# Retention and a spatial-gating block on one core: steps of batches 0 to 2 in another order

## The chip, the core and the metric

The kernel runs on one core of one Trainium2 chip. The core has five engines with a queue of instructions each: TensorE (PE in the profile) for matrix products, VectorE (DVE), ScalarE (ACT), GpSimd (POOL), and SyncE (SP), which here only issues transfers. They wait for each other through semaphores. The metric is the time of one execution in microseconds; before the change its median over three runs is 555.22 us (555.17 to 558.64).

## The reference

Two blocks follow each other. `x` of the second is the output of the first.

```python
# first: q, k, v of (8 batches, 8 heads, 576, 64)
scores = scale * np.matmul(q, k.transpose(0, 1, 3, 2))
Dmat = np.where(rel >= 0, gamma[:, None, None] ** rel[None, :, :], 0.0)
out = np.matmul(scores * Dmat[None], v)                  # rel = i - j, gamma per head
# second: x of (8, 576, 512)
h = np.maximum(x @ w_in, 0.0)
u, v = (h[..., :512], h[..., 512:])
v_n = (v - mean(v)) / np.sqrt(var(v) + 1e-06)            # over the last axis
v_s = np.einsum('ts,bsd->btd', w_spatial, v_n) + b_spatial[None, :, None]
result = (u * v_s) @ w_out
```

## The kernel before, in words

The eight batches go through five stages. **Retention** (`retention(b)`) works a batch in four chunks of 128 positions and a tail of 64: `scores` forms a chunk's products of q and k on TensorE and multiplies them by the decay on VectorE (`at`); `burst` runs the state products, the next chunk's scores and the products with v on TensorE and updates the state `st`; `evac` splits the chunk into a high and a low half in `x`; `prep` scales the keys and queries of a chunk on GpSimd (`qkv`, `qsc`). **v** (`v_steps`) forms five row blocks of v (block 4 is the tail) and normalises each: Relu on ScalarE, statistics on VectorE, the standard deviation and the centring on ScalarE, its inverse on VectorE, the high half of vn on ScalarE, the low half on VectorE. **u** (`u_stage`) forms eight tiles of 128 x 288 with a Relu on ScalarE. **vs** (`vs_stage`) multiplies vn by w_spatial, eight tiles of 14 matmuls, and gates them with u on VectorE. **f** (`f_stage`) multiplies by w_out, eight tiles, which ScalarE copies to `o` and SyncE stores.

Every operand exists as a high and a low half, so each product is three matmuls (`mm3`). The weights come in 64-bit words and are converted while the first batches run: `front` (ScalarE's absolute value and GpSimd's max), `mid` (three operations on VectorE: a shift and two combines on the whole tile `f`), `back` (ScalarE's high half, GpSimd's low half). Kinds 0, 1 and 2 are the u half of w_in, its v half, and w_out, in four pieces each. w_spatial comes as fp32 and is split by `w_sp_steps`: four `wsp` pieces, a cast on ScalarE and a subtraction on GpSimd each, and a last step for the tail (`wtl`), two of each.

Results of TensorE go to PSUM. Two banks (`r`) serve the retention in turn. All other tiles share the pool `ps_m` with four buffers (line 41): a tile holds its buffer from its first matmul to the last operation that reads it, for a v block that is the low half of vn.

What sets the order is of two sorts. Up to `ordered[0] = False` (line 639) the order is written out by hand: generators for v blocks, mids and splits are advanced step by step with `go`, between calls of `scores`, `burst`, `evac`, `prep` and `load`. In this part lie retention of batches 0 and 1, v of batch 0, then for batch 0 vs ahead of u (tile vs (0,0) is gated with `pre`, the Relu of the two u tiles of block 0 that are formed first). Behind it a scheduler places the instructions of each engine by its own times; the program gives it v and u of batch 1, with one step of `wout_work` (front, mid or back of w_out's pieces 2 and 3) at each tile, then f of batch 0, then from `interleave` (line 461) the rest of batch 1 beside the retention of batch 2, and so on with each batch beside the next one's retention. Each engine then runs its queue in that order and waits at an instruction whose input is not ready.

Of the kernel before, what the change touches and what calls it, by code (L numbers as in the profile page):

```python
# [18 lines left out]
B, H, S, D = 8, 8, 576, 64  # L19
# [8 lines left out]
NMB = DM // P  # L28
# [5 lines left out]
def retention_gmlp(ctx, tc, qkv, q_x, qk_t, q_xt, v_t, w_in, w_sp, b_sp, w_out, amask, qscale, kdec, sdec, out):  # L34
# [20 lines left out]
    def slot(name):  # L55
        return cp.tile([P, 2, NCB, S], F32R, name=name, tag="slot", bufs=2)
# [44 lines left out]
    def pair():  # L101
        banks.reverse()
        return banks[0]
# [84 lines left out]
    def front(kind, i, clamp=po):  # L188
        words = staged[kind, i].rearrange("p (n two) -> p n two", two=2)
        hw, lw = words[:, :, 1], words[:, :, 0]  # L190
        f = early[:, i] if kind == 1 else sp.tile([P, 512], F32, name=f"f_{kind}{i}", tag="f", bufs=3)
        a = f if clamp is po else ps_m.tile([P, 512], F32, name=f"w_{kind}{i}", tag="m")
        ac.activation(out=a, in_=hw.bitcast(F32), func=AF.Abs)
        if clamp is po:
            po.tensor_scalar(out=a, in0=a, scalar1=2.0 ** -15, scalar2=None, op0=ALU.max)
        part[kind, i] = hw, lw, a, f
# [15 lines left out]
    def mid(kind, i):  # L212
        for _ in mid_steps(kind, i):
            pass

    def back(kind, i, eng=po):
        hi, lo = (w[:, i, DH:] if kind == 1 else w[:, :, i * P:(i + 1) * P] for w in (win if kind < 2 else wout))
        f, ps = (t if kind == 1 else t.rearrange("p (a n) -> p a n", a=NCB) for t in part[kind, i])
        ac.copy(out=hi, in_=ps)
        if eng is po and kind == 1:  # L220
            ac.copy(out=f, in_=ps)
        eng.tensor_tensor(out=lo, in0=f if eng is po else ps, in1=hi.bitcast(F32), op=ALU.subtract)
# [15 lines left out]
    xs = {}  # L238

    def mm(out, w, r, start, stop):  # L240
        tc.keep_in_program_order(pe.matmul(out, w, r, start=start, stop=stop))
# [4 lines left out]
    def rows(c):  # L246
        return C if c < NC else TL
# [4 lines left out]
    def side(p, i):  # L252
        return i ^ (p % 2)

    def scores(b, c):
        n = rows(c)
        q, k, _, _ = chunk[b, c]
        ps = pair().rearrange("p i (a n) -> p i a n", a=NP)
        for s in range(n // D):
            for p, i in heads:  # L260
                mm(ps[half[s ^ side(p, i)], i, p, s * D:n], k[half[i], p, half[s]], q[half[i], p, s * D:n], True, True)
        a = wk.tile([P, 2, NP, C], F32, name=f"at_{b}_{c}", tag="at")
        ve.tensor_tensor(out=a[:, :, :, :n], in0=ps[:, :, :, :n], in1=am[:, :, :, :n], op=ALU.mult)
        at[b, c] = a

    def prep(b, c):
        n = rows(c)
        if c < NC:
            kh = chunk[b, c][2].rearrange("p (h d) -> p h d", h=H)
            po.tensor_tensor(out=kh, in0=kh, in1=kd.broadcast_to([P, H, D]), op=ALU.mult)  # L270
        if c > 0:
            t = qsc[b, c][:, :, :n]
            po.tensor_tensor(out=t, in0=t, in1=qs[:, :, :n], op=ALU.mult)
# [40 lines left out]
    def evac(b, c):  # L314
        src = xo[b, c]
        t = slice(c * C, c * C + rows(c))
        hi, lo = ((xs[b][:, i, :, t] if c < NC else xt[:, :, i]).rearrange("p (a j) n -> p j a n", j=2) for i in range(2))
        ac.copy(out=hi, in_=src)
        ve.tensor_tensor(out=lo, in0=src, in1=hi.bitcast(F32), op=ALU.subtract)
        if c == NC:  # L320
            po.tensor_copy(out=xs[b][:, :, :, t], in_=xt.rearrange("p a i n -> p i a n"))

    def retention(b):
        if b not in xs:
            xs[b] = slot(f"x_{b}")
        nxt = [(b, c) for c in range(NC + 1)] + [(b + 1, c) for c in range(2)]
        if (b, 0) not in at:
            prep(b, 0)
            scores(b, 0)
        yield 0.95  # L330
        for c in range(NC + 1):
            nx = nxt[c + 1] if nxt[c + 1][0] < B and (b, c) != (1, NC) else None
            if nx:
                prep(*nx)
            burst(b, c, nx)
            evac(b, c)
            if nxt[c + 2:] and nxt[c + 2][0] < B and nxt[c + 2] not in chunk:
                load(*nxt[c + 2])
            yield 2.65

    def mm3(ps, w, r, start, stop):
        pe.matmul(ps, w[0], r[0], start=start, stop=False)
        pe.matmul(ps, w[0], r[1], start=False, stop=False)
        pe.matmul(ps, w[1], r[0], start=False, stop=stop)
# [52 lines left out]
    def u_mm(b, db, t, ps):  # L397
        x = xs[b]
        ts = slice(t * HALF, (t + 1) * HALF)
        for cb in range(NCB):  # L400
            mm3(ps, [win[i][:, cb, db * P:(db + 1) * P] for i in range(2)], [x[:, i, cb, ts] for i in range(2)], cb == 0, cb == NCB - 1)
# [4 lines left out]
    def u_tile(b, db, t):  # L406
        ps = ps_m.tile([P, 512], F32, name=f"u_{b}_{db}_{t}", tag="m")[:, :HALF]
        u_mm(b, db, t, ps)
        u_relu(b, db, t, ps)

    def u_stage(b):
        for db in range(NDB):
            for t in range(2):
                u_tile(b, db, t)
                yield 1.6

    def v_stage(b):
        for sb in range(NC + 1):
            v_block(b, sb)
            yield 2.75 if sb < NC else 1.9  # L420
# [20 lines left out]
    def f_stage(b, g):  # L441
        for t in range(2):
            ts = slice(t * HALF, (t + 1) * HALF)
            for mb in range(NMB):
                o = wk.tile([P, HALF], F32, name=f"o_{b}_{mb}_{t}", tag="o", bufs=4)
                ps = ps_m.tile([P, 512], F32, name=f"f_{b}_{mb}_{t}", tag="m")[:, :HALF]
                for db in range(NDB):
                    mm3(ps, [wout[i][:, db, mb * P:(mb + 1) * P] for i in range(2)], [g[:, i, db, ts] for i in range(2)], db == 0, db == NDB - 1)
                ac.copy(out=o, in_=ps)
                sy.dma_start(out=out[b, mb * P:(mb + 1) * P, ts], in_=o)  # L450
                yield 1.6

    def main(b):
        if b > 1:
            yield from v_stage(b)
            yield from u_stage(b)
        g = slot(f"g_{b}")
        yield from vs_stage(b, g)
        yield from f_stage(b, g)

    def interleave(a, r, ta, tr):
        da = dr = 0.0
        a, r = iter(a), iter(r)
        la = lr = True
        while la or lr:
            if lr and (not la or dr / tr <= da / ta):
                try:
                    dr += next(r)
                except StopIteration:
                    lr = False  # L470
            elif la:
                try:
                    da += next(a)
                except StopIteration:
                    la = False

    def go(gen, n=1):
        for _ in range(n):
            next(gen)
# [32 lines left out]
    v = [v_steps(0, sb) for sb in range(NC + 1)]  # L512
    m = [mid_steps(0, i) for i in range(NDB)]
    sps = w_sp_steps()
# [11 lines left out]
    burst(0, 3, None)  # L526
    go(m[0])
    evac(0, 3)
    go(v[1])
    scores(0, NC)  # L530
    go(v[1])
    go(sps, 2)
    go(v[2], 2)
    burst(0, NC, None)
    evac(0, NC)
    go(v[2])
    go(m[0])
    back(0, 0)
    load(1, 1)
    fetch(2, 0)  # L540
    prep(1, 0)
    go(sps)
    go(v[3])
    go(v[4])
    go(v[3])
    go(v[2], 2)
    go(v[4])
    go(v[3])
    go(sps)
    ret = retention(1)  # L550
    xs[1] = slot("x_1")
    scores(1, 0)
    go(v[4])
    go(v[3])
    go(sps)
    u = cp.tile([P, NDB, S], F32, name="u", tag="u")
    pre = cp.tile([P, NDB, DM], F32, name="pre", tag="wout1")
    for t in range(2):
        ps = ps_m.tile([P, 512], F32, name=f"u_0_0_{t}", tag="m")[:, :HALF]
        u_mm(0, 0, t, ps)  # L560
        ac.activation(out=pre[:, t, :HALF], in_=ps, func=AF.Relu)
        go(v[4 - t])
    go(v[4])
    go(v[3])
    go(ret)

    def vs_tile(t, db):
# [52 lines left out]
    gated_u(1, 1)  # L620
    gated_u(1, 2)
    go(ret)
    mid(2, 1)
    gated_u(1, 3)
    back(2, 1)
    split_g(1)

    def wout_work():
        for i in range(2, NMB):
            front(2, i)  # L630
            yield
            mid(2, i)
            yield
            back(2, i)
            yield

    work = wout_work()
    g0 = xs[0]
# [1 line left out]
    for eng in (pe, ve, ac, po):  # L640
        ctx.enter_context(tc.issue_after(eng.last))

    for stage in (v_stage(1), u_stage(1)):
        for _ in stage:
            next(work, None)
    for _ in f_stage(0, g0):
        pass
    for b in range(1, B):
        interleave(main(b), retention(b + 1) if b + 1 < B else [], 50.0 if b > 1 else 26.1, 12.5 if b > 1 else 13.25)


_OUT = (B, DM, S)
# [74 lines left out]
```

## Time and profile before

| | |
|---|---|
| median of 3 runs | 555.22 us |
| the profiled execution | 555.62 us |
| its span, first to last instruction | 553.70 us |
| TensorE, matmuls busy | 536.8 us (97%) |
| VectorE busy | 269.0 us (49%) |
| ScalarE busy | 207.4 us (37%) |
| GpSimd busy | 133.9 us (24%) |
| mean granted TensorE clock | 0.988 |

Nearly all instructions are issued through one helper, so the profile gives line 71 for them; they are told apart by the names of their tiles (`vs<-wsp,vn` is a matmul of the vs stage that reads wsp and vn). Times are in us from the start of the span. TensorE's clock is given as a share of its full speed. The rows below are of one execution, on its own clock.

### The profile page before, as it was taken

To read this page: it belongs to the slowest core of one execution; us is meant where nothing else is said; L and a number is where in the kernel's file an instruction comes from. 1 tells how busy PE (TensorE), PEld (TensorE's weight loads), DVE (VectorE), ACT (ScalarE), POOL (GpSimd) and SP (SyncE) were. 2 spreads that over 40 slices of the span, in tenths; PEclk is the share of its full clock that TensorE was granted. 3 is DMA by queue.
4 is the path that set the end of the run, shared out by engine and by line. 5 is a ranking of instruction groups with operands and counts; after the bars stand their busy time and mean duration, and the time that the engine had idled before them with its cause. 6 is when DMAs were issued, how large, how long until landed. Compare 5 with 4: busy or idle time off the path is not lost.

```text
span 553.7 us, 15312 instructions
## 1 busy us (share of the span) xinstructions
PE 536.8 (97%) x6735; PEld 498.0 (90%) x6735; DVE 269.0 (49%) x588; ACT 207.4 (37%) x447; POOL 133.9 (24%) x133
## 2 busy tenths in 40 slices
PE   6897999899999999999999999999999999999997
PEld 4676998799998899989999899988999899998997
DVE  7685566922643735247351654327353373506240
ACT  4356323742223632236222551226322362226422
POOL 4747557700212111202112120121201122000000
PEclk8898899999999999999999999999999999999999
DMA  8992465002464322533225222342225342020002
GB/s 318 381 310 80 162 193 191 0 22 76 164 180 146 105 80 67 201 118 102 50 96 182 78 96 50 128 150 89 88 55 180 114 149 49 2 76 11 2 1 86
DMA packets 37045, 64.08 MB, mean 116 GB/s; under 512 B 14833, under 2 KB 27249, under 8 KB 33010
## 3 DMA queue, kind: packets, MB, share of 16 engines
q1 hardware_dynamic: 36978, 63.10, 34.5%
q8 instruction: 53, 0.87, 0.7%
q14 instruction: 14, 0.11, 0.1%
HBM read 53.65 MB, written 9.44 MB: 114 GB/s over the span
## 4 chain that ended last, share of the span: by engine, by line
PE 85%; DMA 5%; DVE 5%; ACT 3%; issue 1%; POOL 1%; SPq 0%; ACTq 0%; DVEq 0%
PE vs L71 21%; PE f L71 19%; PE u L71 17%; PE v L71 14%; PE r L71 14%; DMA qkv<-in_qkv 5%; DVE f L71 2%; DVE s L71 1%; ACT x L71 1%; DVE sm L71 1%; ACT vn L71 0%; POOL qsc L71 0%; DVE vn L71 0%; DVE w L71 0%; POOL qkv L71 0%
## 5 line engine op out<-in xcount | busy, mean ns | idle before, releaser
L71 PE MATMUL vs<-wsp,vn 128*128 128x288 f32 x768 | 115.6, 299 | 3.0 <-ACT pre L71 2.4
L71 PEld LDWEIGHTS vs<-wsp,vn 128*128 128x128 f32 x768 | 105.9, 189 | 4.9 <-ACT pre L71 2.7
L71 PE MATMUL u<-x,win 128*128 128x288 f32 x768 | 105.6, 296 | 2.2 <-ACT u L71 2.2
L71 PEld LDWEIGHTS u<-x,win 128*128 128x128 f32 x768 | 103.0, 188 | 3.7 <-POOL f L71 2.5
L71 PE MATMUL v<-win,x 128*128 128x512 f32 x384 | 93.3, 398 | 0.0
L71 PE MATMUL f<-g,wout 128*128 128x288 f32 x672 | 92.3, 296 | 0.0
L71 PEld LDWEIGHTS f<-g,wout 128*128 128x128 f32 x672 | 89.8, 188 | 0.5
L71 DVE TENSOR_TENSOR at<-r,am 128x1024 f32<-128x1024 f32 (+1 forms) x40 | 44.5, 1113 | 94.0 <-PE r L71 94.0
L71 PEld LDWEIGHTS v<-win,x 128*128 128x128 f32 x384 | 71.0, 188 | 16.6
L71 POOL TENSOR_TENSOR qsc<-qsc,qs 128x512 f32<-128x512 f32 (+1 forms) x31 | 36.1, 1165 | 177.5 <-DMA qsc<-in_q_x 112.7
L71 PEld LDWEIGHTS r<-qkv 64*64 64x64 f32 x2176 | 47.3, 139 | 14.0 <-issue 6.6
L71 PE MATMUL r<-qkv 64*64 64x64 f32 (+1 forms) x2176 | 54.0, 240 | 4.6 <-POOL qkv L71 2.8
L71 DVE BATCH_NORM_STATS2 s<-v 128x6 f32<-128x512 f32 (+1 forms) x40 | 27.7, 693 | 60.3 <-ACT v L71 59.3
L71 ACT COPY o<-f 128x288 f32<-128x288 f32 x64 | 25.6, 400 | 72.0 <-PE f L71 71.9
L71 ACT CAST g<-vs 128x288 fp32r<-128x288 f32 x56 | 22.3, 399 | 75.8 <-DVE vs L71 75.8
L71 ACT CAST x<-r 128x512 fp32r<-128x512 f32 x32 | 18.8, 586 | 60.0 <-DVE st L71 60.0
L71 POOL TENSOR_TENSOR qkv<-qkv,kd 128x512 f32<-128x512 f32 x32 | 33.3, 1043 | 32.3 <-DMA qkv<-in_qkv 25.1
L71 DVE TENSOR_TENSOR g<-vs,g 128x288 fp32r<-128x288 f32 x56 | 25.6, 458 | 26.3 <-ACT g L71 26.3
L71 PE MATMUL r<-at,qkv 64*64 64x64 f32 (+1 forms) x1152 | 37.6, 228 | 0.4 <-DVE at L71 0.4
L71 POOL TENSOR_TENSOR st<-st,sd 128x256 f32<-128x256 f32 x24 | 14.9, 620 | 93.4 <-DVE st L71 93.4
L71 DVE TENSOR_TENSOR vs<-vs,u 128x288 f32<-128x288 f32 x56 | 26.0, 464 | 23.0 <-PE vs L71 23.0
L71 PEld LDWEIGHTS r<-at,qkv 64*64 64x64 f32 (+1 forms) x1152 | 32.1, 141 | 2.8 <-DVE at L71 0.6
(73 smaller groups left out, 509.6 us busy)
## 6 DMA issues: line engine op xcount, KB each, us to landing
qkv<-in_qkv SPq DMA_DIRECT2D x31, 1024.0 KB, 5.3
out<-o SPq DMA_DIRECT2D x64, 144.0 KB, 1.8
qsc<-in_q_x SPq DMA_DIRECT2D x24, 256.0 KB, 3.2
raw_v<-in_w_in SPq DMA_DIRECT2D x4, 512.0 KB, 6.5
qkv<-in_qk_t SPq DMA_DIRECT2D x8, 256.0 KB, 3.2
qkv<-in_v_t SPq DMA_DIRECT2D x16, 128.0 KB, 3.4
raw<-in_w_in SPq DMA_DIRECT2D x4, 512.0 KB, 8.4
raw<-in_w_out SPq DMA_DIRECT2D x4, 512.0 KB, 4.1
```

Source lines behind the costliest of these rows:

```text
L71: ins = op(*args, **kw)
```

## The change

Three things move; no instruction's work changes. First, in the part written by hand: the `wsp` splits and the `wtl` step of w_spatial are advanced earlier, the last steps of v blocks 2, 3 and 4 of batch 0 come in another order, the key scaling of chunk 0 of batch 1 (`prep(1, 0)`) comes later, and that chunk's `scores` move behind the two first u tiles. Second, mid and back of w_out's piece 1 leave the part written by hand, and pieces 1 to 3 now advance with the u tiles of batch 1 alone, no longer from the v blocks on. Third, `main(1)` begins with f of batch 0, so the retention of batch 2 is interleaved with f of batch 0, vs and f of batch 1, instead of the last two.

```diff
     def main(b):
-        if b > 1:
+        if b == 1:
+            yield from f_stage(0, g0)
+        else:
             yield from v_stage(b)
             yield from u_stage(b)
...
     evac(0, 3)
+    go(sps, 2)
     go(v[1])
     scores(0, NC)
     go(v[1])
-    go(sps, 2)
     go(v[2], 2)
     burst(0, NC, None)
     evac(0, NC)
     go(v[2])
+    go(sps)
     go(m[0])
     back(0, 0)
     load(1, 1)
     fetch(2, 0)
-    prep(1, 0)
-    go(sps)
     go(v[3])
     go(v[4])
     go(v[3])
-    go(v[2], 2)
+    go(v[2])
+    go(sps)
+    go(v[4])
+    go(v[2])
+    prep(1, 0)
+    go(v[3])
+    go(sps)
     go(v[4])
     go(v[3])
-    go(sps)
-    ret = retention(1)
-    xs[1] = slot("x_1")
-    scores(1, 0)
-    go(v[4])
-    go(v[3])
-    go(sps)
...
         u_mm(0, 0, t, ps)
+        if t:
+            go(v[4])
+            go(v[3])
         ac.activation(out=pre[:, t, :HALF], in_=ps, func=AF.Relu)
-        go(v[4 - t])
     go(v[4])
     go(v[3])
+    ret = retention(1)
+    xs[1] = slot("x_1")
+    scores(1, 0)
     go(ret)
...
     go(ret)
-    mid(2, 1)
     gated_u(1, 3)
-    back(2, 1)
     split_g(1)

     def wout_work():
-        for i in range(2, NMB):
-            front(2, i)
-            yield
+        for i in range(1, NMB):
+            if i > 1:
+                front(2, i)
+                yield
             mid(2, i)
             yield
             back(2, i)
...
-    for stage in (v_stage(1), u_stage(1)):
-        for _ in stage:
-            next(work, None)
-    for _ in f_stage(0, g0):
+    for _ in v_stage(1):
         pass
+    for _ in u_stage(1):
+        next(work, None)
     for b in range(1, B):
-        interleave(main(b), retention(b + 1) if b + 1 < B else [], 50.0 if b > 1 else 26.1, 12.5 if b > 1 else 13.25)
+        interleave(main(b), retention(b + 1) if b + 1 < B else [], 50.0 if b > 1 else 40.0, 12.5)
```

At two places the engines' order is shown as it stands in the built program. The first is ScalarE at the end of v of batch 0, just before vs tile (0,0). In the names, `v_3` and `v_4` are the v blocks in PSUM, `mv` and `sm` their statistics, `vt` the tail block of vn, `vn_343` the high half of vn. Before:

```order
L71 ACTIVATE v_4_587<-v_4_587,mv_4_636 64x512
L71 ACTIVATE sm_3_645<-mv_3_643,eps 128x1
L71 ACTIVATE v_3_580<-v_3_580,mv_3_643 128x512
L71 CAST wtl_82<-raw_s 1x576
L71 CAST wtl_81<-raw_s 128x576
L71 ACTIVATE pre<-u_0_0_654 128x288
L71 ACTIVATE vt_83<-v_4_587,sm_4_638 64x512
L71 ACTIVATE vt_84<-v_4_587,sm_4_638 64x512
L71 ACTIVATE pre<-u_0_1_674 128x288
L71 ACTIVATE vn_343<-v_3_580,sm_3_645 128x512
```

And in the changed kernel, ScalarE at the same place:

```order
L71 CAST wtl_82<-raw_s 1x576
L71 CAST wtl_81<-raw_s 128x576
L71 ACTIVATE sm_4_623<-mv_4_621,eps 64x1
L71 ACTIVATE v_4_586<-v_4_586,mv_4_621 64x512
L71 ACTIVATE sm_3_630<-mv_3_628,eps 128x1
L71 ACTIVATE v_3_579<-v_3_579,mv_3_628 128x512
L71 ACTIVATE pre<-u_0_0_635 128x288
L71 ACTIVATE vt_83<-v_4_586,sm_4_623 64x512
L71 ACTIVATE vt_84<-v_4_586,sm_4_623 64x512
L71 ACTIVATE vn_343<-v_3_579,sm_3_630 128x512
L71 ACTIVATE pre<-u_0_1_649 128x288
```

The two `wtl` casts moved ahead of the standard deviations, and the second `pre` moved behind vn of block 3.

The second place is VectorE in v of batch 1, which the scheduler orders. `vn_344<-v_1` is the low half of vn of block 1, `f_1271` is w_out's piece 2 before the change and `f_1421` and `f_1471` are its pieces 2 and 3 in the changed kernel. Before:

```order
L71 SCALAR_TENSOR_TENSOR vn_344<-v_0_1244,sm_0_1262,vn_343 128x512
L71 BN_STATS s_1_2_1318<-v_2_1304 128x6
L71 SCALAR_TENSOR_TENSOR vn_344<-v_1_1274,sm_1_1292,vn_343 128x512
L71 BN_AGGR mv_2_1320<-s_1_2_1318 128x2
L71 BN_STATS s_1_3_1347<-v_3_1333 128x6
L71 RECIPROCAL sm_2_1322<-sm_2_1322 128x1
L71 BN_AGGR mv_3_1349<-s_1_3_1347 128x2
L71 TENSOR_SCALAR sm_2_1322<-mv_2_1320,sm_2_1322 128x1
L71 TENSOR_SCALAR f_1271<-f_1271 128x512
```

And in the changed kernel, VectorE behind block 1's reciprocal:

```order
L71 TENSOR_SCALAR f_1421<-f_1421 128x512
L71 TENSOR_SCALAR sm_1_1284<-mv_1_1282,sm_1_1284 128x1
L71 SCALAR_TENSOR_TENSOR f_1421<-raw_942,f_1421 128x512
L71 TENSOR_SCALAR sm_1_1284<-sm_1_1284 128x1
L71 BN_STATS s_1_2_1307<-v_2_1293 128x6
L71 SCALAR_TENSOR_TENSOR f_1421<-raw_942,f_1421 128x512
L71 TENSOR_SCALAR f_1471<-f_1471 128x512
L71 TENSOR_SCALAR sm_1_1284<-sm_1_1284 128x1
L71 BN_AGGR mv_2_1309<-s_1_2_1307 128x2
L71 SCALAR_TENSOR_TENSOR f_1471<-raw_1052,f_1471 128x512 x2
L71 BN_STATS s_1_3_1334<-v_3_1320 128x6
L71 SCALAR_TENSOR_TENSOR vn_344<-v_1_1266,sm_1_1284,vn_343 128x512
```

The mids of pieces 2 and 3 moved from behind the low half of block 1 to ahead of it, and the statistics of block 3 with them.

The third place is GpSimd at the same time. `qkv` and `qsc` are the scalings of `prep` for batch 2, `f` with one operand the max of `front`, `wout_1055` the low half of a piece of w_out. Before:

```order
L71 TENSOR_TENSOR qkv_0_1145<-qkv_0_1145,kd 128x512
L71 TENSOR_TENSOR qkv_1_1217<-qkv_1_1217,kd 128x512
L71 TENSOR_TENSOR qsc_1_1219<-qsc_1_1219,qs 128x512
L71 TENSOR_SCALAR f_1271<-f_1271 128x512
L71 TENSOR_TENSOR qsc_2_1733<-qsc_2_1733,qs 128x512
L71 TENSOR_SCALAR f_1360<-f_1360 128x512
```

And in the changed kernel, GpSimd from chunk 0's scaling on:

```order
L71 TENSOR_TENSOR qkv_0_1145<-qkv_0_1145,kd 128x512
L71 TENSOR_SCALAR f_1421<-f_1421 128x512
L71 TENSOR_SCALAR f_1471<-f_1471 128x512
L71 TENSOR_TENSOR qkv_1_1217<-qkv_1_1217,kd 128x512
L71 TENSOR_TENSOR wout_1055<-f_1087,wout_1054 128x4x128
L71 TENSOR_TENSOR qsc_1_1219<-qsc_1_1219,qs 128x512
L71 TENSOR_TENSOR qsc_2_1618<-qsc_2_1618,qs 128x512
```

Both maxima moved ahead of the scalings of chunks 1 and 2, and the low half of w_out's piece 1 (`f_1087`) moved in between from ahead of the splits of batch 0's gated tile.

## Rows read from the trace of the kernel before

**Rows 1.** The page, busy time of each engine, share of the span, instructions.

```profile
PE 536.8 (97%) x6735; PEld 498.0 (90%) x6735; DVE 269.0 (49%) x588; ACT 207.4 (37%) x447; POOL 133.9 (24%) x133
```

**Rows 2.** Timeline of PE: start, length, operation, count [idle before, what ended it].

```profile
44.41 3.45 PE L71 MATMUL u<-x,win 128*128 128x288 f32 x24
50.28 1.46 PE L71 MATMUL vs<-wsp,vn 128*128 128x288 f32 x9 [2.42 <-ACT pre L71]
...
54.09 2.41 PE L71 MATMUL r<-qkv 64*64 64x64 f32 x64
...
57.91 2.20 PE L71 MATMUL vs<-wsp,vn 128*128 128x288 f32 x12
...
134.50 1.36 PE L71 MATMUL r<-qkv 64*64 64x64 f32 x64
...
136.64 1.86 PE L71 MATMUL vs<-wsp,vn 128*128 128x288 f32 x12
```

**Rows 3.** Windows: stretch, length, busy of PE, PEld, DVE, ACT, POOL, PEclk, DMA.

```profile
52.00:56.00 4.00, 3.71 (x61) 3.15 (x65) 1.35 (x3) 0.24 (x1) 2.48 (x3) 0.50 0.00 0
56.00:60.00 4.00, 4.00 (x65) 3.77 (x58) 2.08 (x3) 1.42 (x3) 0.61 (x1) 0.67 0.21 37
104.00:108.00 4.00, 1.76 (x14) 1.55 (x13) 4.00 (x10) 2.80 (x6) 2.53 (x3) 1.00 0.00 0
```

**Rows 4.** Timeline of ACT at the end of v of batch 0.

```profile
48.56 1.36 ACT L71 CAST wtl<-raw_s 1x576 fp32r<-1x576 f32 x2
49.83 0.40 ACT L71 ACTIVATE pre<-u 128x288 f32<-128x288 f32 x1
50.13 1.24 ACT L71 ACTIVATE vt<-v,sm 64x512 fp32r<-64x512 f32 x2
...
51.56 0.68 ACT L71 ACTIVATE vn<-v,sm 128x512 fp32r<-128x512 f32 x1
```

**Rows 5.** Timeline of DVE at the end of v of batch 0.

```profile
44.84 1.21 DVE L71 TENSOR_TENSOR at<-r,am 128x1024 f32<-128x1024 f32 x1
...
52.27 0.75 DVE L71 SCALAR_TENSOR_TENSOR vn<-v,sm,vn 128x512 fp32r<-128x512 f32 x1
```

**Rows 6.** Timeline of PE in u of batch 1.

```profile
103.46 1.75 PE L71 MATMUL u<-x,win 128*128 128x288 f32 x12
107.45 11.52 PE L71 MATMUL u<-x,win 128*128 128x288 f32 x84 [2.24 <-ACT u L71]
```

**Rows 7.** Timeline of ACT, the Relu of u tile 0_0 of batch 1.

```profile
106.90 0.40 ACT L71 ACTIVATE u<-u 128x288 f32<-128x288 f32 x1
```

**Rows 8.** Timeline of DVE, mids of weight pieces, and v of batch 1.

```profile
61.72 0.83 DVE L71 TENSOR_SCALAR f<-f 128x512 int32<-128x512 int32 x1 [1.46 <-POOL f L71]
...
78.70 1.42 DVE L71 SCALAR_TENSOR_TENSOR f<-raw,f 128x512 int32<-128x512 int32 x2
...
91.20 1.80 DVE L71 SCALAR_TENSOR_TENSOR f<-raw,f 128x512 int32<-128x512 int32 x1
...
101.36 0.69 DVE L71 BATCH_NORM_STATS2 s<-v 128x6 f32<-128x512 f32 x1
101.97 0.74 DVE L71 SCALAR_TENSOR_TENSOR vn<-v,sm,vn 128x512 fp32r<-128x512 f32 x1
...
103.61 1.48 DVE L71 TENSOR_SCALAR f<-f 128x512 int32<-128x512 int32 x1
```

**Rows 9.** Timeline of POOL beside those operations of VectorE.

```profile
60.20 2.94 POOL L71 TENSOR_SCALAR f<-f 128x512 f32<-128x512 f32 x2 [0.64 <-ACT f L71]
...
89.46 2.99 POOL L71 TENSOR_TENSOR x<-u,x 128x576 fp32r<-128x576 f32 x2
92.40 1.07 POOL L71 CAST x<-xt 128x512 fp32r<-128x512 f32 x1
...
98.77 2.05 POOL L71 TENSOR_TENSOR qkv<-qkv,kd 128x512 f32<-128x512 f32 x2
...
103.48 1.32 POOL L71 TENSOR_TENSOR qsc<-qsc,qs 128x512 f32<-128x512 f32 x1
```

## The prediction

> **What bounds the kernel now.** I read the page's busy times first. TensorE is busy for 536.8 of 553.7 us [rows 1], so a new order can win at most the 16.9 us in which it waits, and what it loses at a low clock. Then TensorE's timeline, for where it waits; then the windows, for the clock granted there; then the timelines of ScalarE, VectorE and GpSimd, for what each wait hangs on. Two places matter, both early. At the first, TensorE has finished the u tiles of batch 0 and stands until 50.28 for vs tile (0,0); the wait of 2.42 us ends with ScalarE's `pre` [rows 2]. Of the two clock levels (2.4 and 1.2 GHz) the lower one is granted right after: 0.50 in 52 to 56 and 0.67 in 56 to 60, so half until about 56 + 4 x 0.33 / 0.5 = 58.6 [rows 3]. At the second, u tile 0_1 of batch 1 waits 2.24 us for the Relu of u tile 0_0 [rows 6]; the clock stays at 1.00 there [rows 3]. Behind it TensorE works to the end without a wait worth naming, so time won or lost before 119 us is kept to the end.
>
> **First place, term 1: tile vs 0_0 ends earlier.** ScalarE ran the two `wtl` casts from 48.56, `pre` of tile 0 at 49.83, the two vt scalings at 50.13, `pre` of tile 1, and vn of block 3 at 51.56 [rows 4]. `pre` of tile 0 is what frees the PSUM buffer that vs 0_0 takes; vn of block 3 and VectorE's low half behind it, 52.27 to 53.02 [rows 5], are what its last matmuls need. In the changed order the casts stand ahead of the statistics and `pre` of tile 1 behind vn. So `pre` starts 49.83 - 48.56 = 1.27 earlier, at 48.56, and vn of block 3 another 0.30 earlier (one `pre`, 49.83 to 50.13): 50.0. VectorE's low half then ends at 53.02 - 1.57 = 51.45. The casts don't lengthen the queue ahead, since two wsp casts go into time in which ScalarE stood idle before block 1's vn. Behind the low half come one vs matmul and the two of the tail, 3 x 1.86 / 12 = 0.47 at full clock (the tile at 136.64 [rows 2]): about 51.95 instead of 54.09. Term 1: **-2.1**. Bounds: -1.3 (only the casts) and -2.6 (the earlier Relu of block 2 moves the rest forward, too).
>
> Two things could eat it. The chunk scores (1,0) now run behind the u tiles; their product on VectorE, 1.21 long at 44.84 [rows 5], comes after block 3's low half, so at 52.65, and the scores of chunk 1 write the same PSUM bank. TensorE reaches them after the state products, half of the 1.36 at 134.50 [rows 2], at about 51.95 + 0.7, so this is covered; if it isn't, up to 0.6 is lost. On GpSimd the split of w_in's piece 0 stands one wsp split later, all of them starting earlier; TensorE's u tile meets it while vs 0_0 is not yet possible, so some tenths there cost nothing.
>
> **First place, term 2: the clock.** From 54.09 to 57.91 the burst of chunk 0 took 3.82 at the low clock; the same burst one batch later takes 136.64 - 134.50 = 2.14 at full clock, and the vs tile behind it 1.86 instead of 2.20 [rows 2]. With one wait of 2.4 replaced by several of about 0.5, I take it that the clock doesn't fall: 1.68 + 0.34, **-2.0**. Nearest row: with the wait of 2.24 at the second place it didn't fall. If it does fall: 6.6 us at half speed, 6.6 x (1 - 2.14 / 3.82) = 2.9 lost again. Bounds: -2.0 and +0.9.
>
> **Second place, term 3: a new wait.** The four PSUM buffers of `ps_m` go to the next tile as they come free. v blocks 0 to 3 of batch 1 fill them, v 4 takes block 0's, and u 0_0 takes block 1's, which is freed by the low half of vn for block 1 on VectorE. Before, this ended at 101.97 + 0.74 = 102.71, ahead of u 0_0 at 103.46 [rows 6, 8]: no wait. In the changed order (the second place in the section on the change) the mids of pieces 2 and 3, six operations on whole tiles, and two statistics stand between block 1's reciprocal and that low half.
>
> What do six such operations cost? Alone they take 0.71 (78.70, two in 1.42). They are longer while GpSimd runs an operation with two SBUF inputs: the shift at 103.61 ended at 105.09, 0.29 after GpSimd's qsc (103.48 to 104.80); the combine at 91.20 ended at 93.00, 0.55 after GpSimd's x (to 92.45), and the copy behind on GpSimd, 1.07, was drawn out by it [rows 8, 9]. Beside a max a shift does not wait to the end: at 61.72 it took 0.83, while GpSimd's two maxima, 1.47 each, ran from 60.20 to 63.14 [rows 8, 9]. So, but for the max, each waits for the GpSimd operation that it finds running, and then the next GpSimd operation waits for it. In the changed kernel GpSimd has no gap here (the third place). On the clock of before (the shift from the first place left out): copy to 93.47, the last combine of piece 1 to 94.0, the two x splits (2 x 1.45) to 96.9, chunk 0's scaling (1.03) to 97.9, max of piece 2 (1.47) to 99.4, max of piece 3 to 100.85. VectorE's shift of piece 2 starts at 99.4 and takes 0.83 beside the max (100.2), its combine the same, an estimate from that row (101.1), statistics 0.69 (101.8); the next combine meets chunk 1's scaling (to 101.9) and ends at 102.45; the shift of piece 3 meets wout's split (1.3 as a qsc scaling of its shape, to 103.75) and ends at 104.05; the two combines meet the two qsc scalings (1.30 each) and end at 105.9 and 107.75. Statistics 0.69, low half 0.74: 109.2, so u 0_0 starts there instead of at 103.46: **+5.7**.
>
> Bounds: with all six alone, 99.4 + 6 x 0.71 + 2 x 0.69 + 0.74 = 105.8, a wait of 2.3. From above: each of them waits a whole GpSimd operation, the max too: 100.85 + 0.29, then five rounds of 1.03 to 1.32 plus 0.29 or 0.55, the two statistics and the low half: about 111.3, a wait of 7.8. I stay at 5.7, since it uses each row for the pair of operations that it shows. The Trainium skill says on its page "SBUF — State Buffer" (Who interferes with whom) that VectorE and GpSimd share a port pair as an exclusive lock, held for a whole instruction, whoever comes second blocking fully. Taken for every pair of operations, it gives the upper bound, and 2.1 us more than my sum; the qsc and x rows agree with it, the 0.83 beside the max does not.
>
> **Term 4:** u 0_1 still waits for u 0_0's Relu, which is now ready to run at once: 0.55 from the Relu's start (106.90 [rows 7]) to u 0_1, and an estimated 0.35 from TensorE's end to the Relu: 0.9 instead of 2.24, **-1.3**. **Term 5:** a TensorE wait of 5.7 will, by the first place's fall after 2.42, take the clock down. All of the fall would cost 2.9; part of it lies in the wait itself, so I take half, **+1.5** (bounds 0 and 2.9).
>
> **At no cost:** the third retention along f of batch 0. It is the same work for TensorE, which has no wait there; VectorE does nothing in f of batch 0 before, and that is the cover. If it were gone, a burst would wait for one product of 1.21. On SyncE the load of chunk 2 now stands ahead of the store of o tile 2_0; it waits for the burst that TensorE runs just before f tile 2_0, so the store isn't held up, and four `o` buffers stand behind it. Wout's pieces are complete by about 110, and f 1_0 of batch 0 needs piece 1 past 119.
>
> **Sum.** The profiled execution took 555.62 (span 553.70), 0.40 above the median of 555.22. 555.62 - 2.1 - 2.0 + 5.7 - 1.3 + 1.5 = 557.4; on the median's level **557.0**. What the first place gives, the second takes back.
>
> **Rivals.** (a) The new wait is short: GpSimd's order leaves VectorE alone and the clock holds. 555.2 - 4.1 + 2.3 - 1.3 = 552.1, faster. For it: the combines at 78.70 took 0.71. Against: five GpSimd operations in a row wait in its queue. (b) The clock falls at the first place all the same, since the waits there remain, by the times above, at some 0.6 ahead of the tile and 1 us in it: 557.0 + 2.9 = 559.9, slower. It decides if 0.50 shows anywhere from 48 to 60. (c) The lock holds for all pairs: 557.0 + 2.1 = 559.1. (d) u 0_0 gets another buffer and doesn't wait: 555.2 - 4.1 - 1.3 = 549.8. Against it: the buffers are taken in the order of release, which explains before's waits at both places.
>
> **Chances.** Forecast 0.48 (its own range 555.2 to 558.8), (a) 0.22, (b) 0.14, (c) 0.10, (d) 0.06. The range 551.8 to 560.5 leaves out (d), the low end of (a) and the high end of (b). A change under 1% (5.55 us) can't be told from none; faster than 549.7 is half of (d) and little else, 0.04; slower than 560.8 is part of (b) and of (c) with the whole fall of the clock, 0.08; the rest 0.88.
>
> **What would show it.** Right: vs 0_0 starts within 0.3 us of `pre`'s end near 48.5, granted clock 1.00 from 48 to 60, the vs tile 1_0 about 4 us earlier; then one TensorE wait of 4 to 7 us ahead of u 0_0 of batch 1, ended by VectorE's vn, with a low clock behind it. Wrong: no wait there, one under 3 us, or a low clock at the first place.

## The result and the profile after

Over 13 executions each, run in turn on one chip, the changed kernel takes 558.55 us (556.34 to 562.6) and the kernel before 555.17 (554.26 to 558.64): a ratio of 1.0068, 95% interval 1.005 to 1.0085. The profiled execution of the changed kernel is the fastest of its 13, 556.34 with a span of 554.6. One execution among all those reported below, of e4, took 1787.51 us and is left out of its median. The busy times of the changed kernel's profiled execution:

```profile
PE 533.7 (96%) x6735; PEld 496.1 (89%) x6735; DVE 272.1 (49%) x588; ACT 207.8 (37%) x447; POOL 135.1 (24%) x133
```

Two rows of the kernel before that the readings below need: v block 2 of batch 0, and the second wait in vs tile 0_0, columns as in [rows 2].

```profile
33.68 3.06 PE L71 MATMUL v<-win,x 128*128 128x512 f32 x12
...
52.29 1.40 PE L71 MATMUL vs<-wsp,vn 128*128 128x288 f32 x3 [0.54 <-ACT vn L71]
```

The changed kernel's timeline of PE at both places:

```profile
33.13 3.06 PE L71 MATMUL v<-win,x 128*128 128x512 f32 x12
...
43.52 3.19 PE L71 MATMUL u<-x,win 128*128 128x288 f32 x22 [0.92 <-POOL win L71]
...
48.06 1.46 PE L71 MATMUL vs<-wsp,vn 128*128 128x288 f32 x9 [0.53 <-ACT pre L71]
49.78 0.53 PE L71 MATMUL vs<-wsp,vn 128*128 128x288 f32 x2 [0.26 <-ACT vn L71]
50.77 0.40 PE L71 MATMUL vs<-wsp,vn 128*128 128x288 f32 x1 [0.46 <-DVE vn L71]
...
51.36 1.43 PE L71 MATMUL r<-qkv 64*64 64x64 f32 x64
...
53.58 1.86 PE L71 MATMUL vs<-wsp,vn 128*128 128x288 f32 x12
...
104.89 3.25 PE L71 MATMUL u<-x,win 128*128 128x288 f32 x12 [6.60 <-DVE vn L71]
108.79 11.39 PE L71 MATMUL u<-x,win 128*128 128x288 f32 x84 [0.65 <-ACT u L71]
```

At the first place the wait for `pre` is 0.53 instead of 2.42 [rows 2]. The waits for vn of block 3 inside the tile are 0.26 and 0.46, where one of 0.54 was. A wait of 0.92 for GpSimd's split of w_in is new, ahead of the tile. It delays nothing by itself: u tile 0_0 of batch 0, half of the row at 43.52, was done near 45, and ScalarE came to its `pre` at 47.61. At the second, u tile 0_0 of batch 1 waits 6.60 for VectorE's low half of vn block 1, where before it didn't wait [rows 6]. ScalarE at the first place, with `pre` of tile 0 ending at 48.01 and TensorE starting at 48.06:

```profile
47.61 0.40 ACT L71 ACTIVATE pre<-u 128x288 f32<-128x288 f32 x1
```

The windows, columns as in [rows 3]: the clock (the third figure from the end) is 1.00 from 52 to 60, where it was 0.50 and 0.67, and falls in the new wait instead.

```profile
52.00:56.00 4.00, 4.00 (x86) 3.87 (x83) 2.54 (x4) 1.76 (x4) 0.76 (x2) 1.00 0.35 82
56.00:60.00 4.00, 4.00 (x66) 3.83 (x68) 2.21 (x3) 1.65 (x5) 2.80 (x2) 1.00 0.62 250
100.00:104.00 4.00, 0.00 (x0) 0.00 (x0) 3.97 (x6) 1.81 (x4) 3.02 (x2) 0.68 0.00 0
104.00:108.00 4.00, 3.11 (x12) 2.90 (x12) 3.95 (x15) 2.84 (x6) 1.26 (x1) 0.50 0.00 0
108.00:112.00 4.00, 3.35 (x25) 3.24 (x25) 1.49 (x6) 2.98 (x7) 0.00 (x0) 0.97 0.00 0
```

What VectorE does around TensorE's wait from 98.29 to 104.89 (its timeline; the first row is block 1's reciprocal, `f` are the mids of w_out's pieces 2 and 3, the last row is the low half that ends the wait):

```profile
95.15 0.15 DVE L71 RECIPROCAL sm<-sm 128x1 f32<-128x1 f32 x1
95.22 0.46 DVE L71 TENSOR_SCALAR f<-f 128x512 int32<-128x512 int32 x1
...
95.72 1.40 DVE L71 SCALAR_TENSOR_TENSOR f<-raw,f 128x512 int32<-128x512 int32 x1
...
97.77 1.05 DVE L71 SCALAR_TENSOR_TENSOR f<-raw,f 128x512 int32<-128x512 int32 x1
98.75 1.48 DVE L71 TENSOR_SCALAR f<-f 128x512 int32<-128x512 int32 x1
...
100.37 3.20 DVE L71 SCALAR_TENSOR_TENSOR f<-raw,f 128x512 int32<-128x512 int32 x2
...
104.10 0.73 DVE L71 SCALAR_TENSOR_TENSOR vn<-v,sm,vn 128x512 fp32r<-128x512 f32 x1
```

And GpSimd beside it (the first row is the two maxima, to 95.39):

```profile
92.45 2.94 POOL L71 TENSOR_SCALAR f<-f 128x512 f32<-128x512 f32 x2
95.36 1.21 POOL L71 TENSOR_TENSOR qkv<-qkv,kd 128x512 f32<-128x512 f32 x1
96.54 1.74 POOL L71 TENSOR_TENSOR wout<-f,wout 128x512 fp32r<-128x512 f32 x1
98.23 3.12 POOL L71 TENSOR_TENSOR qsc<-qsc,qs 128x512 f32<-128x512 f32 x2
101.32 1.70 POOL L71 TENSOR_TENSOR wout<-f,wout 128x512 fp32r<-128x512 f32 x1
```

The two engines take turns. The first combine (to 97.12) ends 0.55 behind the key scaling (to 96.57), the second (to 98.82) 0.54 behind wout's low half (to 98.28), the last (to 103.57) 0.55 behind the next one (to 103.02). GpSimd pays as well: the key scaling takes 1.21 instead of 1.03, the query scalings 1.56 each instead of 1.30 ([rows 9], in the prediction's sum), wout's low halves 1.74 and 1.70 instead of 1.28 in e3 below.

### The profile page after: what moved, and what is told of

It is laid out like the page before. It is cut to its first block, busy times and chain, and to the rows that moved or that the text cites. A ratio compares the mean times of both kernels' runs of the same rounds, so it can differ in the third digit from the quotient of the medians.

```text
span 554.6 us, 15310 instructions
## 1 busy us (share of the span) xinstructions
PE 533.7 (96%) x6735; PEld 496.1 (89%) x6735; DVE 272.1 (49%) x588; ACT 207.8 (37%) x447; POOL 135.1 (24%) x133
## 4 chain that ended last, share of the span: by engine, by line
PE 87%; DVE 4%; DMA 4%; ACT 2%; issue 1%; POOL 1%; SPq 0%; ACTq 0%
PE vs L71 22%; PE f L71 19%; PE u L71 18%; PE v L71 14%; PE r L71 14%; DMA qkv<-in_qkv 4%; DVE f L71 2%; DMA raw<-in_w_out 1%; DVE s L71 1%; ACT v L71 1%; DVE sm L71 0%; DVE w L71 0%; DVE vn L71 0%; ACT wtl L71 0%; POOL qsc L71 0%
## 5 line engine op out<-in xcount | busy, mean ns | idle before, releaser
L71 PE MATMUL u<-x,win 128*128 128x288 f32 x768 | 107.2, 299 | 8.2 <-DVE vn L71 6.6
L71 PEld LDWEIGHTS u<-x,win 128*128 128x128 f32 x768 | 104.3, 190 | 10.2 <-DVE vn L71 7.0
L71 PEld LDWEIGHTS r<-qkv 64*64 64x64 f32 x2176 | 45.8, 135 | 13.8 <-issue 6.3
L71 PE MATMUL r<-qkv 64*64 64x64 f32 (+1 forms) x2176 | 52.3, 235 | 5.4 <-POOL qkv L71 3.5
L71 ACT ACTIVATE u<-u 128x288 f32<-128x288 f32 x56 | 22.4, 408 | 34.3 <-PE u L71 34.1
```

Of the source, the lines that this page charges most:

```text
L71: ins = op(*args, **kw)
```

## The experiments

Two theories were put against each other, with variants. One is the forecast's: the first place wins some 4 us, and the second loses more than that because the mids of w_out stand on VectorE ahead of the low half that frees u 0_0's buffer; the wait takes the clock down. The other: the loss comes from another part of the change, or the clock is what costs. Ratios are to the kernel before, run in turn with each experiment; its medians were 554.82 (e1 to e4), 555.15 (e5 to e8) and 554.95 (e9 to e11).

**e1, the first move alone.** Only the steps written by hand are in their new order; w_out's pieces and the third retention are as before.

```diff
     evac(0, 3)
+    go(sps, 2)
     go(v[1])
     scores(0, NC)
     go(v[1])
-    go(sps, 2)
...
+        if t:
+            go(v[4])
+            go(v[3])
         ac.activation(out=pre[:, t, :HALF], in_=ps, func=AF.Relu)
-        go(v[4 - t])
```

> Before, with only the part written by hand in its new order (w_spatial's splits, last v steps of batch 0, the scores of batch 1's chunk 0 behind the u tiles). Theory M (the first place gains about 4 us, the whole loss is at the second place, u 0_0 of batch 1): no wait over 1 us at the first place, vs 1_0 about 4.3 us earlier than before, u 0_0 of batch 1 without a wait, time 551 to 552 against 555.2. Rival R1 (what the first place gains is given back whatever stands behind it): 555. Rival R2 (in most runs the clock falls at the first place, which the one profile of the changed kernel did not catch): gain under 2 us, time 553.5, and a mean clock below 0.988.

Measured: 556.19 us, ratio 1.0015 (0.9994 to 1.0035). The theory expected 551 to 552, and no gain is in the time. The first place has it: the waits there are those of the changed kernel, 0.92, 0.53, 0.26 and 0.46, and the clock is 1.00 from 44 to 64. But the second place got worse by this move alone (PE, then ScalarE):

```profile
100.49 1.75 PE L71 MATMUL u<-x,win 128*128 128x288 f32 x12
105.52 3.22 PE L71 MATMUL u<-x,win 128*128 128x288 f32 x12 [3.29 <-ACT u L71]
109.30 12.13 PE L71 MATMUL u<-x,win 128*128 128x288 f32 x72 [0.56 <-ACT u L71]
```

```profile
103.55 0.30 ACT L71 ACTIVATE sm<-mv,eps 128x1 f32<-128x1 f32 x1 [2.23 <-DVE sm L71]
...
104.97 0.41 ACT L71 ACTIVATE u<-u 128x288 f32<-128x288 f32 x1
```

The wait for u 0_0's Relu, 2.24 in [rows 6], is 3.29: on ScalarE the Relu stands behind block 3's standard deviation, whose statistics come late from VectorE, where the first operations of piece 2's mid stand ahead of them. The clock falls in this wait (0.53 and 0.50 from 104 to 112), so the next 12 matmuls take 3.22. In this profile, of the slowest of the ten executions (558.03), the gain can be seen won and lost. From v block 2 of batch 0 (at 35.85 here) to u 0_0 of batch 1 it takes 100.49 - 35.85 = 64.64, against 103.46 - 33.68 = 69.78 before, so 5.1 less. From there to the end of u it takes 121.43 - 100.49 = 20.94 against 15.51, so 5.4 more: 1.6 of waits, and 3.8 because the 96 matmuls take 17.10 instead of 13.27. What follows: earlier work at the first place moved the scheduler's order at the second, and the same mids held up another operation.

**e2, the third move alone.**

```diff
-        if b > 1:
+        if b == 1:
+            yield from f_stage(0, g0)
+        else:
             yield from v_stage(b)
...
-    for _ in f_stage(0, g0):
-        pass
...
-        interleave(main(b), ..., 50.0 if b > 1 else 26.1, 12.5 if b > 1 else 13.25)
+        interleave(main(b), ..., 50.0 if b > 1 else 40.0, 12.5)
```

> Before, with only the third move: the retention of batch 2 along f of batch 0, vs and f of batch 1. Theory M: no change, 555.2 within 1 us, waits at both places as before (2.4 and 2.2). Rival R3 (the retention beside f of batch 0 costs what the one profile does not show, some 2 us): 557.

Measured: 554.14 us, ratio 0.9983 (0.9966 to 1.0001), with the waits of before at both places (2.43 and 2.26). The third move is worth nothing that can be told.

**e9, the second move alone.**

```diff
-    mid(2, 1)
...
-    back(2, 1)
...
-        for i in range(2, NMB):
-            front(2, i)
-            yield
+        for i in range(1, NMB):
+            if i > 1:
+                front(2, i)
+                yield
...
-    for stage in (v_stage(1), u_stage(1)):
-        for _ in stage:
-            next(work, None)
+    for _ in v_stage(1):
+        pass
+    for _ in u_stage(1):
+        next(work, None)
```

> The second move alone, with VectorE's order as it then falls out: the low half of vn block 1 stands behind one shift of w_out's piece 2 only, the other five mids behind it. Theory (the wait ahead of u 0_0 is as long as the mids that stand ahead of that low half; the second move in itself costs nothing): first place as before; at u 0_0 a wait of 0 to 2.5 us, at u 0_1 up to 2.5, in sum about what before waits there (2.2) or 1 more, 554 to 557. Rival (moving w_out's pieces to the u tiles costs the same wherever the low half stands): a wait of 5 or more at u 0_0, 560 to 563, the first place's loss and the new wait together.

Measured: 558.84 us, ratio 1.0066 (1.0042 to 1.0089), as slow as the whole change. The theory's 554 to 557 missed, and so did the rival, both with its 560 to 563 and with its place. Its PE and ScalarE, in the slowest of the ten executions (561.39):

```profile
103.53 1.85 PE L71 MATMUL u<-x,win 128*128 128x288 f32 x12 [0.43 <-DVE vn L71]
109.48 12.94 PE L71 MATMUL u<-x,win 128*128 128x288 f32 x84 [4.10 <-ACT u L71]
```

```profile
106.50 0.62 ACT L71 CAST wout<-f 128x512 fp32r<-128x512 f32 x1 [2.29 <-DVE f L71]
...
108.94 0.40 ACT L71 ACTIVATE u<-u 128x288 f32<-128x288 f32 x1
```

u 0_0 hardly waits, since its low half stands early, as expected. But its Relu stands on ScalarE behind the cast of a w_out piece, which waits 2.29 for VectorE's combine, and behind block 3's centring, which waits for VectorE too. Together the two waits are 4.53 instead of 2.24, with the low clock behind them; from u 0_0 to the end of u it takes 18.89 against 15.51. This execution also waits 0.88 and 0.84 for loads at 156 and 172, which the kernel before doesn't in its profile. So the low half of block 1 is only one of the things that the mids can hold up; to look at that buffer alone, as the prediction did, was enough for the changed kernel and too little for this one. Nor do the moves add up: alone they measured +1.4 (e1, not clear of noise), -0.7 (e2, not clear of noise) and +3.9, together +3.4, because e1 and e9 each got another order at the second place from the scheduler.

**e3, the changed kernel with the mids behind all low halves of batch 1 on VectorE.**

```diff
-        ve.tensor_scalar(out=fi, in0=a.bitcast(I32), scalar1=3, ...)
+        ins = ve.tensor_scalar(out=fi, in0=a.bitcast(I32), scalar1=3, ...)
+        if kind == 2 and not ordered[0]:
+            tc.keep_in_program_order(ins)
...
-        ve.scalar_tensor_tensor(out=lo, in0=ps, scalar=nrstd, ...)
+        ins = ve.scalar_tensor_tensor(out=lo, in0=ps, scalar=nrstd, ...)
+        if b == 1:
+            tc.keep_in_program_order(ins)
```

> The changed kernel, with the mids of w_out's pieces 1 to 3 held behind all low halves of vn of batch 1 in VectorE's order. Theory M: the wait of 6.6 us ahead of u 0_0 goes, and with it the low clock behind it; one wait under 1.5 us in u of batch 1 is left; time 550 to 551.5. Rival R4 (the work on VectorE is too much at this place in any order, so the wait moves to a later u tile or, for w_out, to f of batch 0): a wait of 3 us or more there, time 555 or more.

Measured: 547.73 us, ratio 0.9867 (0.9837 to 0.9897). Its PE at the second place:

```profile
98.04 12.90 PE L71 MATMUL u<-x,win 128*128 128x288 f32 x96
```

No wait is left, the clock is 1.00, and the 96 matmuls of u run through in 12.90. From the end of v to the end of u it took 118.97 - 103.46 = 15.51 before [rows 6] and 120.18 - 98.29 = 21.89 in the changed kernel. This is faster than both kernels, and than the 550 to 551.5 of the theory.

**e7, the same without the third move, and e8, the same without the first and third.** The edits are the diffs above put together: those of e1, e9 and e3 for e7, those of e9 and e3 for e8. Lines that both share with e3:

```diff
+        if kind == 2 and not ordered[0]:
+            tc.keep_in_program_order(ins)
```

> The first and second move without the third, with the mids of w_out's pieces 1 to 3 behind all low halves of batch 1 on VectorE. Theory: no wait at u 0_0 and the clock at 1.00 at both places, as in e3; the third move is worth nothing but the cover for w_out's pieces, so 547.5 to 549, at most one wait of about 0.5 us ahead of an f tile of batch 0. Rival (the third retention along f is what makes room for the late mids): f tiles 1_0 to 3_0 of batch 0 wait for w_out by 2 us or more in sum, 550 to 552.

> The second move alone with the mids of w_out's pieces 1 to 3 behind all low halves of batch 1 on VectorE; the part written by hand up to vs tile 0_0 and the third retention are those of before. Theory (two places, each with its own price): the first place is as before, a wait of 2.4 for pre and a low clock from 52 to 58; the wait of 2.24 at u 0_1 falls to under 1: 552 to 553. Rival (what e3 won lies all at the second place): 548 to 549.

Measured: e7 548.39 us, ratio 0.9876 (0.9859 to 0.9893); e8 552.18, ratio 0.9949 (0.9926 to 0.9971). Both are what the theory gave. e7 less e8 is the first move by itself, 548.39 - 552.18 = **-3.8** (the intervals of the two ratios leave about 1.6 to either side); e8 less before is the wait at the second place and what hung on it, **-3.0**. In part the wait of 2.24 was the mids' work already in the kernel before: the Relu of u 0_0 stands on ScalarE behind vn of block 2, which waits for an operation that VectorE has behind the shift at 103.61 [rows 8] and a combine (ScalarE before):

```profile
106.32 0.69 ACT L71 ACTIVATE vn<-v,sm 128x512 fp32r<-128x512 f32 x1 [1.18 <-DVE sm L71]
```

e7 beside e3 shows once more that the third move gives next to nothing. The profiled execution of e8 is its fastest, 549.01 (the other four: 551.2 to 554.1), and holds a surprise, here its PE and one window:

```profile
49.63 1.46 PE L71 MATMUL vs<-wsp,vn 128*128 128x288 f32 x9 [2.42 <-ACT pre L71]
```

```profile
52.00:56.00 4.00, 3.74 (x107) 3.28 (x106) 2.37 (x4) 0.37 (x1) 1.85 (x2) 1.00 0.01 4
```

The wait for `pre` is the one of before to the hundredth, and the clock didn't fall behind it. The mean clock of that execution is 0.994, that of the other four 0.981 to 0.984, so in those it was low for longer; where, no trace shows.

**e4, the changed kernel with GpSimd's query and key scalings of batch 2, chunks 1 and 2, cut to one head group of the tile.** The rest of these scalings is left out; every engine keeps its order.

```diff
+        w = 1 if (b, c) in ((2, 1), (2, 2)) else None
...
-            kh = chunk[b, c][2].rearrange("p (h d) -> p h d", h=H)
+            kh = chunk[b, c][2].rearrange("p (h d) -> p h d", h=H)[:, :w]
...
-            t = qsc[b, c][:, :, :n]
+            t = qsc[b, c][:, :w, :n]
```

> The changed kernel with every engine's order kept, but GpSimd's scalings of batch 2, chunks 1 and 2, cut to an eighth of the keys and a quarter of the queries (the rest stays unscaled), so that three GpSimd operations of 1.0 to 1.3 us beside VectorE's mids become 0.2 to 0.4. Theory M (each mid operation waits for the GpSimd operation that it meets): the six mid operations fall from 7.6 us in sum to about 5, the wait ahead of u 0_0 from 6.6 to about 4, the time by 2 to 3 us. Rival R5 (the mid operations are that long by themselves, or the order alone makes the wait): the sum stays above 7, the wait at 6.6, no change of time.

Measured: 557.46 us, ratio 1.0038 (1.0015 to 1.0062), against 1.0068 (1.005 to 1.0085) for the changed kernel. By the ratios that is 1.7 us faster, by the medians 0.7, and the intervals overlap: less than the 2 to 3 that were expected, and not clear of noise. The trace is clearer. Its mids on VectorE, and the wait on PE:

```profile
95.61 0.46 DVE L71 TENSOR_SCALAR f<-f 128x512 int32<-128x512 int32 x1
...
96.11 0.69 DVE L71 SCALAR_TENSOR_TENSOR f<-raw,f 128x512 int32<-128x512 int32 x1
...
97.45 1.06 DVE L71 SCALAR_TENSOR_TENSOR f<-raw,f 128x512 int32<-128x512 int32 x1
98.43 0.68 DVE L71 TENSOR_SCALAR f<-f 128x512 int32<-128x512 int32 x1
...
99.24 2.40 DVE L71 SCALAR_TENSOR_TENSOR f<-raw,f 128x512 int32<-128x512 int32 x2
```

```profile
102.95 3.25 PE L71 MATMUL u<-x,win 128*128 128x288 f32 x12 [4.29 <-DVE vn L71]
```

The six mids sum to 5.29 instead of 7.59, 2.30 less, and the wait is 4.29 instead of 6.60, 2.31 less. So what the mids lose the wait loses, one to one, and a third of it hung on these scalings of GpSimd.

**e6, the changed kernel with the wait filled.** 24 matmuls on data that stands idle, between v block 4 and u 0_0.

```diff
+            if b == 1:
+                for _ in range(24):
+                    spins.append(pe.matmul(banks[1][:, 0], wsp[0][:, 0, :P], wsp[0][:, 0, :512], start=True, stop=True))
...
+            if (b, db, t, cb) == (1, 0, 0, 0):
+                behind(ins, spins[-1])
```

> The changed kernel, with 24 matmuls of 128x512 on idle data put on TensorE between v block 4 and u tile 0_0 of batch 1, into a retention bank that is free then; all other engines keep their order. They fill about 5.7 of the 6.6 us of the wait and move nothing else. Theory (the wait is VectorE's, and the clock falls because TensorE stands still in it): u 0_0 starts at the same time as without them, within 0.3 us, after a wait of under 1.2; the granted clock stays at 1.00 from 96 to 116; the time falls by what the clock cost, 1.5 to 4 us, to 554 to 556, and less spread between executions. Rival (the clock's fall costs little, and the 558.5 comes from elsewhere): 557.5 to 559.

Measured: 556.71 us (555.83 to 557.86), ratio 1.0029 (1.0016 to 1.0043), against 558.29 for the changed kernel in turn with it. Its PE, ScalarE and one window:

```profile
98.19 5.60 PE L71 MATMUL r<-wsp 128*128 128x512 f32 x24
105.05 1.85 PE L71 MATMUL u<-x,win 128*128 128x288 f32 x12 [1.26 <-DVE vn L71]
108.27 11.46 PE L71 MATMUL u<-x,win 128*128 128x288 f32 x84 [1.37 <-DVE mv L71]
```

```profile
111.06 1.06 ACT L71 ACTIVATE u<-u 128x288 f32<-128x288 f32 x3
```

```profile
104.00:108.00 4.00, 1.85 (x12) 1.61 (x12) 3.94 (x14) 3.44 (x7) 1.28 (x1) 1.00 0.00 0
```

u 0_0 starts at the time of before the filling (105.05, 104.89), so the wait is VectorE's; the clock stays at 1.00, and u 0_0 takes 1.85 instead of 3.25. The time falls by 1.6, at the low end of the 1.5 to 4 that were expected, and 556.71 lies between the theory's 554 to 556 and the rival's 557.5 to 559. One reason is that u 0_1 now waits 1.37 instead of 0.65. The edit moved ScalarE's order too: the Relus of the first three u tiles stand together at 111.06, where the changed kernel has that of u 0_0 at 108.23. So u 0_1 can't wait for that Relu here; its wait ends with VectorE, which finishes block 2's low half at 108.12 and the next operation, `mv`, at 108.21. In the two profiles u 0_0 to the end of u is 14.68 here and 15.29 in the changed kernel, 0.6 apart: 1.3 of clock less 0.7 of wait. The 1.6 between the medians fits the larger prices of the clock in e10 and e11 below. The executions run from 555.83 to 557.86, those of the changed kernel in turn with it from 556.41 to 559.27.

**e5, e10 and e11, the changed kernel again,** to see where executions longer than the profiled one spend their time.

> The changed kernel once more, unaltered, to see where its clock is low in an execution other than the one shown. Theory: the low clock lies where it lay, at the opening (up to 20 us) and behind the wait ahead of u tile 0_0 of batch 1 (from about 102 on), where it lasts longer than until 108 in an execution that is slower by 1 to 4 us; 1.00 from 48 to 60. Rival (b) of the prediction: in a typical execution the clock falls at the first place too, so that 0.50 shows somewhere between 48 and 60. Time under both 556 to 561.

> The changed kernel unaltered, one profile, to see where an execution above the shown 556.34 spends its time. Theory: wait at u 0_0 again 6.6 within 0.1; the excess lies in the stretches of low clock (opening up to 28 us, and behind the wait from 100 on) and in tenths of a us of waits for the load of chunk 2 of batch 1 near 69. Rival (b): 0.50 between 48 and 60.

> As e10, a further profile of the changed kernel: the same rows are looked for, the low clock at the opening, at 48 to 60 and from 100 to 120, and the wait near 69.

Measured: e5 558.29 us over 8 executions, ratio 1.005 (1.0032 to 1.0068), the profiled one 557.77; e10 558.89 and e11 559.47, one execution each. In all three u 0_0 waits 6.60 or 6.61, and the clock is 1.00 from 44 to 64: rival (b) of the prediction is out. What differs is how long the clock stays low behind the wait. PE and a window of e11:

```profile
105.63 3.25 PE L71 MATMUL u<-x,win 128*128 128x288 f32 x12 [6.60 <-DVE vn L71]
109.53 13.78 PE L71 MATMUL u<-x,win 128*128 128x288 f32 x84 [0.65 <-ACT u L71]
```

```profile
108.00:112.00 4.00, 3.35 (x14) 3.03 (x14) 2.22 (x8) 1.70 (x4) 0.00 (x0) 0.50 0.00 0
```

The 96 matmuls take 3.25 + 11.39 = 14.64 in the first profile, 14.63 in e5 (3.25 + 11.38), 16.44 in e10 (3.25 + 13.19) and 17.03 in e11 (3.25 + 13.78), against 1.85 + 11.46 = 13.31 in e6. So the clock costs 1.3, 1.3, 3.1 and 3.7 there. The rest lies in the opening, which no move touches (the first u tiles start between 43.5 and 44.4, the clock is low somewhere between 8 and 24), and in e5 in a wait of 0.60 for a load at 70.

## Why the prediction was right, and where it wasn't

It gave 557.0 and reckoned that a change under 1% can't be told from none. The kernel takes 558.55, inside the range and 1.55 above the forecast; the ratio of 1.0068 is under 1%, though its interval leaves out no change. The mechanism was right at both places, and what was off were sizes, those of terms 3 and 5 above all. By its steps:

- **Term 1 (-2.1) held.** vs 0_0 ended at 51.36 instead of 54.09. Of these 2.73, TensorE was 0.55 ahead before the place was reached (v block 2 at 33.13, in the profile of before at 33.68), by a shorter opening; 2.2 is left.
- **Term 2 (-2.0) held in the profiles, and rests on chance.** The burst takes 53.58 - 51.36 = 2.22 instead of 3.82, the vs tile 1.86 instead of 2.20 [rows 2]: 1.94 together. Yet e8 shows an execution with the old wait and no fall, so the kernel before may not pay it in every execution either. Terms 1 and 2 together, over executions, are e7 less e8: -3.8, against -4.1 forecast.
- **Term 3 (+5.7) was right in its mechanism and 0.9 short: 6.60.** The mids were priced well in sum, 7.66 against 7.59 measured, from rows of other pairs of operations. Singly they were off both ways (the first shift 0.83 against 0.46, the first combine 0.9 against 1.40), since the first combine met the key scaling and no longer a max, so part of that agreement is luck. The stretch from the first of them to the end of the low half came out, too: 9.8 forecast, 104.83 - 95.22 = 9.61. The step that was mis-sized is its start. The prediction let the first shift begin when GpSimd's max was done, 4.06 ahead of TensorE's end of v (103.46 - 99.4). But it stands on VectorE behind block 1's reciprocal, which came at 95.15, and it began at 95.22, 3.07 ahead of TensorE's end of v (104.89 - 6.60 = 98.29).
- **Term 4 (-1.3) held:** 0.65 instead of 0.9 to wait, so -1.6.
- **Term 5 (+1.5) was mis-sized, as was its bound.** The four profiles give 1.3, 1.3, 3.1 and 3.7, 2.35 in the mean. The bound of 2.9 took over how long the clock had been low at the first place in one execution; behind a longer wait it was low longer, and differently from one execution to the next.
- **The third move (0) held** (e2, e7). So did the remark that the later split of w_in costs nothing: its wait was 0.92, more than "some tenths", and covered.

Put together with what was measured: 555.17 - 3.8 + 6.6 - 1.6 + 2.35 = 558.7, and 558.55 was the result. The forecast's sum differs from this by 0.3 in the first place, 0.9 in term 3, -0.3 in term 4 and 0.85 in term 5.

Of the rivals, (a) and (d) fall with the wait of 6.60, and (b) with the clock of 1.00 at the first place in four profiles. (c) named a lock for every pair of operations. For GpSimd's operations with two inputs the changed kernel agrees with it: each combine ends 0.54 or 0.55 behind one, the shift at 98.75 ends 0.44 behind a query scaling (98.23 to 99.79), and e4 confirms it from the other side. Beside a max it doesn't hold. The shift at 95.22 took 0.46, no longer than without company (0.43), though the max ran to 95.39; the two overlap for 0.17 only, so this row says little. The kernel before says more, VectorE and GpSimd:

```profile
105.20 0.90 DVE L71 SCALAR_TENSOR_TENSOR f<-raw,f 128x512 int32<-128x512 int32 x1
```

```profile
104.74 1.69 POOL L71 TENSOR_SCALAR f<-f 128x512 f32<-128x512 f32 x1
```

This combine took 0.90 and ended at 106.10, while the max ran on to 106.43; in e1 a combine (102.70) took 0.67 inside a max (101.78 to 103.45). So the prediction's rule, a lock for all but the max, is what the rows bear out, and (c) gave 7.8 because it made the first shift wait behind the second max. The Trainium skill, on its page "SBUF — State Buffer" (Who interferes with whom), leaves out of the lock VectorE instructions that have at most one SBUF input and are in none of its two-port modes. That can't explain the combine, which reads two operands from SBUF; by the traces what GpSimd runs beside it counts as well.

What stays open: why the clock stays low for a different time in executions of one program. On its page "TensorE: Matmul & The Clock Gate" (Part 1) the Trainium skill says that the gate's rhythm runs free of the kernel, so that the same program can meet it at another point; the spread of 1.3 to 3.7 fits, and no run here shows it. Nor was it tried what e1 would take with its mids behind the low halves and w_out's steps left on the v tiles.

## What to carry to other kernels

When deferrable work (here the conversion of a later weight) shares an in-order engine with what frees the next tile's buffer, look at all that is queued behind it, there and on the engines that wait for it, and pin it behind the last operation that TensorE needs: this alone was worth 10.8 us here (558.55 to 547.73), nearly three times what the order written by hand won. A scheduler's order at one place moves when work at another comes earlier, so a gain won by hand has to be looked for again in the next stage's queues. Price a wait from where its chain can start, and the clock behind it from several executions.

## What the hardware showed that was not expected

- The same wait can take the clock down or not. Behind 2.42 or 2.43 us it fell in before, in e2 and in e9 (0.50 to 0.53 from 52 to 56) and not in e8; behind 2.24 and 2.26 (before and e2, second place) it didn't; behind 3.29, 4.10, 4.29 and 6.60 it did each time.
- Matmuls on idle data through a wait of 6.60 kept the clock at 1.00 in the profiled execution, and the executions lie closer together: 2.0 us from end to end over 10, against 2.9 over 8 of the changed kernel in the same turn.
- Two engines that take turns on their operands both slow down. In e3, where the mids run late, piece 1's shift takes 0.43 (106.20) and its two combines 1.42 (106.66), with GpSimd idle, so six such operations 3.7 in sum; in the changed kernel they took 7.59, and GpSimd's operations beside them 0.18 to 0.46 longer each.
